# Laying out an attention kernel's instructions with measured durations and a new table of limits

## The chip, the cores and the metric

The kernel runs on one core of one Trainium2 chip. The metric is the time of one execution on the device in microseconds (us). The 48 executions of the kernel before that were taken beside the experiments lie between 832.57 and 835.77 us, all within 0.3% of their median (833.86), and all times compared here are of undisturbed ("fast") runs. One first execution of the kernel before, beside the result, took 1873.47 us and is left out of every comparison.

Short names in what follows: PE is the engine that runs the matmuls (PEld its weight loads, which overlap them: busy for 35% beside PE's 95%), ACT the one that runs most of the exponentials here, DVE and POOL the two that run the elementwise operations, SP the one that starts most transfers. "Line" numbers such as L1563 are those of the kernel's source.

## The reference

Two attention branches over the same input, mixed by a gate. Branch A is dense softmax attention with 2048 positions and 32 heads of width 20. Branch B looks at 8 positions, its own and 7 earlier ones, with a step of 2.

```python
def reference(A_x, A_wqkv, A_wo, B_x, B_wqkv, B_wo, gate_w):
    # _A_ref: q, k, v from x @ wqkv, 32 heads of 20
    #     p = softmax(q k^T * 20 ** -0.5);  (p v) @ wo
    # _B_ref: the same, but each position attends to idx = pos - 2 * (0..7)
    x = A_x                                   # [1, 2048, 640] bf16
    g = _sigmoid((x * gate_w).sum(-1, keepdims=True))
    a = _A_ref(x, A_wqkv, A_wo)
    b = _B_ref(x, B_wqkv, B_wo)
    return g * a + (1 - g) * b
```

Branch A sets the time (its visits, defined below, hold ACT for 790.7 of 831.5 us): 32 heads of 2048 x 2048 exponentials, cut into 2048 "tiles" of 128 x 512.

## The kernel before

Three notions carry everything below.

- A **visit** is one ACT instruction that exponentiates two or three score tiles from a score bank into `ebuf`.
- A **ride** is a tile that rides along in a visit's bank (or in a side bank), but is exponentiated by DVE: one operation makes `uD`, and for each group of up to four rides three shifted copies `eD` follow. PE then multiplies `uD` and the three copies with scaled values.
- A **filler** is a group of four matmuls that adds zeros or writes to a bank nobody reads. It is there to keep PE busy where PE has nothing to do; the granted clock with more and with fewer of them is measured in e4_hold_all (0.999 to 1.000) and e11_fewer_fillers (0.997 in two of four runs).

All instructions are put in order when the kernel is built, by an arithmetic that carries a clock for each engine. It decides at each step what comes next from where these clocks stand. It saves no instruction by itself: it only decides which tile becomes a ride, how many tiles a visit has and what stands between two visits. The durations and delays in the listing are what the layout assumes, not measurements.

```python
LAT = {"pe": 0.22, "act": 0.18, "dve": 0.13, "pool": 0.15, "sp": 0.1}   # assumed: end of a producer to start of a consumer, us
SWITCH = 0.11                                                         # assumed: PE changes its tiling

# in _Sched.task: the modelled start and end of an instruction
start = self.avail[stream]
for d in t.deps:
    start = max(start, d.end + LAT[d.stream])
# [cut: a rule for DVE beside POOL, PE's switch, transfers]
t.end = start + dur
self.avail[stream] = t.end

dvc = lambda n, mode=1: 0.10 + n * 1.0417e-3 / mode      # a generic DVE operation
actc = lambda n: 0.08 + n * 0.8334e-3                    # an ACT operation

# a visit
exps[s] = T("act", actc(512 * n), lambda e: e.activation(
    ebuf[s % NE][:, 0:512 * n], score[s % 2][:, 0:512 * n], ACTF.Exp, scale=LN2 / STEP), ...)

# a ride
t = T("dve", 0.69, lambda e: e.tensor_scalar(
    uD[d % 2][:, 512 * i:512 * (i + 1)].bitcast(I16), side[rb], UOFF, 0.0, op0=ALU.add, op1=ALU.max), ...)

# the shifted copies of a group of n rides, k = 1, 2, 3
T("dve", 0.11 + 0.1334 * n, lambda e, k=k, sl=sl: e.tensor_scalar(
    eD[:, sl % NS, 0:512 * n].bitcast(I16), uD[d % 2][:, 0:512 * n].bitcast(I16), SHIFTS[k], None, op0=ALU.add), ...)

# may the next tile ride?
idle = max(now, exps[s - 2].end + LAT["act"] if s > 1 else 0.0) + 0.4 - sch.avail["dve"]
if idle < -DWAIT:
    return None
# [cut: further conditions]

# side work and fillers of PE until the visit before has ended, plus a slack
lim = (exps[s - 1].end if s >= 1 else sch.avail["act"]) + SLACK[max(0, len(us) - 2)]
spend(lim)
```

The names `SLACK`, `DWAIT` and 17 more come from a table `PLAN`. A row takes effect at the visit whose number is its key and holds until the next row. The table before has 54 rows:

```python
PLAN = {
    0: ((0.32, 0.63), 0.32, 2.5, 2.5, 0.49, -1.0, -0.1, 11.8, 7.0, 7.2, 0.52, 0.47, 4.4, 4.0, 0.0, 0.85, 2, 5.5, 0.0),
    # [cut: 52 rows]
    720: ((0.37, 0.6), 0.13, 2.5, 1.0, 1.23, -1.03, -0.57, 12.37, 5.5, 8.26, 0.66, 0.46, 4.28, 4.75, 0.05, 0.72, 1, 0.0, 0),
}
```

Of the kernel before, what the change touches and what calls it, by code (L numbers as in the profile page):

```python
# [50 lines left out]
    0: ((0.32, 0.63), 0.32, 2.5, 2.5, 0.49, -1.0, -0.1, 11.8, 7.0, 7.2, 0.52, 0.47, 4.4, 4.0, 0.0, 0.85, 2, 5.5, 0.0),  # L51
    10: ((0.3, 0.64), 0.31, 2.5, 2.5, 0.49, -1.0, -0.1, 11.8, 7.0, 7.2, 0.52, 0.47, 4.4, 4.0, -0.32, 0.85, 2, 5.5, 0.0),
    20: ((0.3, 0.64), 0.27, 2.5, 1.0, 0.49, -1.0, -0.1, 11.8, 7.0, 9.93, 0.66, 0.47, 4.4, 4.0, -0.32, 0.85, 2, 5.5, 0.0),
    40: ((0.3, 0.61), 0.27, 2.5, 2.5, 1.15, -0.61, -0.1, 9.38, 7.0, 6.43, 0.52, 0.26, 4.34, 4.91, 0.0, 0.85, 3, 5.5, 0.0),
    60: ((0.27, 0.64), 0.29, 6.6, 6.3, 0.54, -1.02, -0.42, 9.46, 6.2, 6.34, 0.52, 0.47, 4.34, 2.59, 0.0, 0.85, 2, 2.5, 0.0),
    70: ((0.27, 0.64), 0.29, 6.6, 6.3, 0.54, -1.02, -0.42, 9.46, 4.5, 6.34, 0.52, 0.47, 4.34, 5.79, 0.0, 0.69, 2, 2.5, 1),
    80: ((0.27, 0.64), 0.29, 2.5, 6.3, 0.54, -0.4, -0.42, 9.38, 5.5, 6.34, 0.52, 0.47, 4.34, 2.59, 0.0, 0.85, 2, 2.5, -1.5),
    100: ((0.31, 0.7), 0.38, 2.5, 6.3, 0.54, -1.26, -0.42, 9.38, 5.5, 6.34, 0.52, 0.35, 4.34, 2.59, 0.0, 0.85, 2, 2.5, -1.5),
    120: ((0.27, 0.64), 0.33, 6.6, 6.3, 0.54, -1.02, -0.42, 9.46, 4.5, 8.77, 0.52, 0.46, 4.66, 5.79, 0.0, 0.65, 2, 2.5, -3),
    140: ((0.27, 0.64), 0.31, 6.3, 1.0, 0.54, -1.02, -0.42, 9.46, 4.5, 6.56, 0.52, 0.46, 3.47, 5.79, 0.0, 0.65, 1, 9.0, 0),  # L60
    150: ((0.25, 0.55), 0.31, 6.6, 1.0, 0.54, -1.02, -0.42, 9.65, 6.7, 6.56, 0.52, 0.46, 4.34, 5.79, 0.0, 0.65, 2, 9.0, 0),
    160: ((0.33, 0.47), 0.31, 6.6, 1.0, 0.54, -1.02, -0.42, 9.65, 5.5, 6.56, 0.52, 0.46, 4.34, 5.79, 0.0, 0.65, 1, 9.0, -3),
    170: ((0.33, 0.47), 0.31, 6.6, 1.0, 0.88, -1.02, -0.42, 9.65, 5.5, 6.56, 0.52, 0.46, 4.34, 2.17, 0.0, 0.65, 1, 0.0, -3),
    180: ((0.33, 0.47), 0.31, 6.6, 1.0, 0.88, -1.02, -0.42, 9.65, 5.5, 6.72, 0.52, 0.46, 4.34, 2.17, 0.0, 0.65, 1, 0.0, -1.5),
    200: ((0.33, 0.47), 0.31, 6.6, 1.0, 0.88, -1.02, -0.42, 9.65, 5.5, 9.72, 0.52, 0.46, 4.34, 2.17, 0.0, 0.65, 1, 0.0, -1.5),
    210: ((0.34, 0.46), 0.33, 2.5, 1.0, 0.63, -1.02, -0.42, 9.52, 7.0, 8.49, 0.68, 0.46, 5.15, 5.79, 0.0, 0.71, 2, 0.0, -3),
    240: ((0.34, 0.46), 0.35, 2.5, 1.0, 0.63, -1.02, -0.42, 9.74, 6.2, 6.12, 0.68, 0.46, 4.48, 5.79, 0.0, 0.77, 2, 6.6, -3),
    250: ((0.34, 0.46), 0.35, 2.5, 1.0, 0.63, -1.02, -0.42, 9.74, 6.2, 6.12, 0.68, 0.52, 4.48, 5.79, 0.0, 0.77, 2, 6.6, -3),
    260: ((0.34, 0.46), 0.33, 2.5, 1.0, 0.63, -1.02, -0.42, 9.52, 4.5, 8.49, 0.62, 0.46, 4.86, 5.79, 0.0, 0.61, 1, 6.6, -3),
    270: ((0.34, 0.46), 0.39, 1.0, 1.0, 0.63, -1.19, -0.42, 9.92, 6.2, 6.12, 0.68, 0.46, 4.48, 5.79, 0.0, 0.77, 2, 6.6, -3),  # L70
    290: ((0.34, 0.46), 0.39, 1.0, 1.0, 0.63, -1.19, -0.42, 12.33, 6.2, 6.12, 0.68, 0.37, 4.56, 5.88, 0.0, 0.77, 2, 6.6, -3),
    310: ((0.36, 0.5), 0.39, 1.0, 1.0, 0.65, -1.19, -0.42, 12.82, 6.2, 6.12, 0.68, 0.46, 4.48, 5.79, 0.0, 0.77, 2, 6.6, -3),
    320: ((0.36, 0.5), 0.39, 1.0, 6.6, 0.65, -1.19, -0.42, 9.92, 6.2, 7.5, 0.64, 0.46, 4.48, 5.79, 0.0, 0.77, 2, 6.6, -3),
    340: ((0.36, 0.5), 0.39, 1.0, 6.6, 0.61, -1.19, -0.42, 9.92, 6.2, 7.5, 0.68, 0.46, 4.48, 5.79, 0.0, 0.77, 2, 6.6, -3),
    350: ((0.36, 0.5), 0.05, 1.0, 6.6, 0.65, -1.19, -0.42, 10.62, 6.2, 7.5, 0.68, 0.46, 4.48, 5.79, 0.0, 0.77, 2, 6.6, -3),
    360: ((0.36, 0.5), 0.05, 1.0, 6.6, 0.65, -1.19, -0.04, 10.62, 4.5, 7.5, 0.68, 0.46, 4.48, 5.79, 0.0, 0.77, 1, 6.6, -3),
    380: ((0.34, 0.53), 0.05, 1.0, 6.6, 0.65, -1.19, -0.04, 10.62, 4.5, 7.5, 0.68, 0.46, 4.44, 5.79, 0.1, 0.77, 1, 6.6, -3),
    390: ((0.37, 0.49), 0.39, 1.0, 6.6, 0.65, -1.19, -0.42, 9.92, 6.2, 10.01, 0.68, 0.46, 4.48, 5.79, 0.0, 0.76, 2, 6.6, -3),
    400: ((0.42, 0.45), 0.39, 1.0, 2.5, 0.65, -1.19, -0.42, 9.92, 6.2, 10.01, 0.68, 0.46, 4.48, 5.79, 0.0, 0.76, 2, 6.6, -3),
    410: ((0.34, 0.53), 0.05, 1.0, 6.6, 0.65, -1.37, 0.11, 9.38, 4.5, 7.5, 0.68, 0.46, 4.44, 5.79, 0.1, 0.77, 2, 6.6, -3),  # L80
    420: ((0.3, 0.63), 0.07, 1.0, 6.6, 0.65, -1.19, -0.04, 10.62, 4.5, 7.5, 0.68, 0.46, 4.44, 2.04, 0.1, 0.77, 1, 9.0, -3),
    430: ((0.3, 0.63), 0.16, 1.0, 6.6, 0.65, -1.19, -0.95, 11.07, 7.0, 7.5, 0.68, 0.46, 4.44, 2.44, 0.1, 0.77, 1, 9.0, -3),
    460: ((0.3, 0.63), 0.16, 1.0, 1.0, 0.65, -1.51, -0.95, 11.07, 7.0, 9.31, 0.68, 0.46, 4.44, 2.44, 0.2, 0.77, 1, 2.5, 0),
    480: ((0.3, 0.63), 0.16, 1.0, 1.0, 0.65, -1.51, -0.95, 11.07, 7.0, 9.31, 0.68, 0.46, 4.44, 2.44, 0.2, 0.77, 1, 9.0, 0),
    490: ((0.35, 0.6), 0.07, 2.5, 6.6, 1.12, -0.96, -0.04, 12.37, 6.2, 7.85, 0.63, 0.46, 3.76, 5.79, 0.04, 0.67, 1, 5.5, 0),
    500: ((0.35, 0.6), 0.07, 2.5, 6.6, 1.12, -0.96, -0.57, 12.37, 6.2, 7.85, 0.63, 0.46, 4.28, 5.79, -0.03, 0.67, 1, 5.5, 0),
    510: ((0.35, 0.6), 0.07, 2.5, 6.6, 1.12, -0.96, -0.57, 12.37, 6.2, 7.85, 0.63, 0.46, 4.28, 5.79, -0.03, 0.67, 1, 0.0, -3),
    530: ((0.35, 0.6), 0.07, 2.5, 6.6, 1.12, -0.96, -0.57, 15.73, 6.2, 7.85, 0.63, 0.46, 4.28, 5.79, -0.03, 0.67, 1, 0.0, -3),
    540: ((0.35, 0.6), 0.07, 2.5, 6.6, 1.12, 0.16, -0.57, 15.73, 6.2, 7.85, 0.63, 0.46, 3.25, 5.79, -0.03, 0.67, 1, 0.0, -3),
    550: ((0.35, 0.6), 0.07, 2.5, 6.6, 1.12, -0.8, -0.57, 12.37, 6.2, 7.85, 0.6, 0.46, 4.28, 4.89, 0.05, 0.67, 1, 0.0, -3),  # L90
    560: ((0.34, 0.61), 0.07, 6.6, 6.6, 1.12, 0.16, -0.57, 15.73, 6.2, 7.26, 0.63, 0.44, 3.25, 3.16, -0.03, 0.67, 1, 2.5, -3),
    570: ((0.35, 0.62), 0.07, 6.6, 6.6, 1.12, 0.07, -0.57, 15.73, 6.2, 7.26, 0.36, 0.44, 3.25, 3.16, -0.03, 0.67, 1, 2.5, -3),
    580: ((0.35, 0.6), 0.07, 6.6, 6.6, 1.12, -0.96, -0.57, 12.37, 6.2, 7.85, 0.63, 0.46, 4.28, 5.79, -0.47, 0.76, 2, 0.0, -3),
    600: ((0.35, 0.6), 0.07, 2.5, 6.3, 1.12, -0.96, -0.57, 12.37, 6.2, 7.85, 0.63, 0.54, 4.28, 5.79, -0.47, 0.76, 2, 0.0, -3),
    610: ((0.3, 0.64), 0.32, 2.5, 2.5, 0.49, -1.0, -0.1, 11.17, 7.0, 7.2, 0.56, 0.47, 4.4, 3.16, 0.0, 0.85, 2, 5.5, 0.0),
    630: ((0.34, 0.56), 0.07, 2.5, 5.5, 1.12, -0.8, -0.57, 12.37, 6.2, 9.39, 0.69, 0.7, 4.28, 4.89, 0.05, 0.72, 1, 0.0, -3),
    640: ((0.37, 0.58), 0.07, 2.5, 5.5, 1.23, -0.95, -0.57, 12.37, 5.5, 10.86, 0.6, 0.46, 4.28, 4.89, 0.05, 0.72, 1, 0.0, -3),
    650: ((0.36, 0.58), 0.07, 2.5, 5.5, 1.12, -0.8, -0.57, 12.37, 6.2, 9.39, 0.6, 0.55, 4.28, 3.81, 0.09, 0.72, 1, 0.0, 0),
    670: ((0.35, 0.55), 0.07, 2.5, 5.5, 1.12, -0.8, -0.57, 8.92, 6.2, 9.39, 0.6, 0.55, 4.28, 3.81, 0.09, 0.72, 1, 0.0, 0),
    680: ((0.37, 0.6), 0.13, 2.5, 1.0, 1.6, -0.95, -0.57, 12.37, 4.5, 8.26, 0.44, 0.52, 4.29, 4.47, 0.05, 0.72, 1, 0.0, -3),  # L100
    690: ((0.37, 0.6), 0.13, 6.6, 1.0, 1.23, -0.95, -0.38, 12.37, 5.5, 8.26, 0.4, 0.43, 4.28, 4.47, 0.05, 0.76, 1, 0.0, 0),
    700: ((0.37, 0.6), 0.13, 6.3, 1.0, 1.6, -0.95, -0.57, 12.37, 5.5, 8.26, 0.54, 0.52, 6.07, 4.47, 0.05, 0.72, 2, 0.0, -3),
    710: ((0.26, 0.61), 0.13, 2.5, 1.0, 1.23, -0.95, -0.39, 12.37, 5.5, 8.26, 0.66, 0.59, 4.28, 4.47, 0.05, 0.72, 1, 0.0, 0),
    720: ((0.37, 0.6), 0.13, 2.5, 1.0, 1.23, -1.03, -0.57, 12.37, 5.5, 8.26, 0.66, 0.46, 4.28, 4.75, 0.05, 0.72, 1, 0.0, 0),
}
WEIGHTS = (1.0, 0.83984375, 0.70703125, 0.59375)
UOFF = 15992.765
K = len(SHIFTS)



LAT = {"pe": 0.22, "act": 0.18, "dve": 0.13, "pool": 0.15, "sp": 0.1}
SWITCH = 0.11
# [211 lines left out]
def _build(ctx, nc, A_x, A_wqkv, A_wo, B_wqkv, B_wo, gate_w, out):  # L325
# [1060 lines left out]

    BT0 = 230.0
    BT1 = 860.0
    BALL = 170.0
    DIDLE2 = -0.1  # L1390

    DWAIT = 0.49
# [410 lines left out]
```

## Time and profile before

| the kernel before | value |
|---|---|
| time, median of undisturbed runs | 833.5 us |
| span of the profiled run | 831.5 us |
| ACT busy, PE busy, DVE busy | 96%, 95%, 82% |
| visits (of three, two, one tile) | 726 (270, 455, 1) |
| tiles on ACT + rides | 1721 + 327 = 2048 |
| filler groups | 197 |

The prediction below shows the engine shares, the groups and the account of ACT. Two further views matter. The first is the chain of work that ended last, by line. Each share is the part of the span that the chain, followed back from the last instruction, spent in that line:

```profile
ACT ebuf L1563 44%; PE score L1540 12%; PE obank L1608 10%; PE side L562 9%; PE score L562 4%; PE obank L1629 1%; DVE eD L802 1%; PE score L1236 1%; PE obank L464 1%; ACT eB L919 1%; PE score L1629 0%; PE side L1629 0%; PE side L1259 0%; DVE uD L1553 0%; ACT tB L953 0%
```

The second is the list of waits: who waited, at which line, for whom, the sum in us, how often, and the longest.

```profile
PEld score L1540 <- ACT ebuf L1563: 142.8, 346, 1.2
...
PEld score L1540 <- DVE uD L1553: 20.5, 43, 0.9
...
PEld score L1540 <- DVE eD L802: 13.6, 34, 0.5
...
ACT ebuf L1563 <- PE score L1540: 7.9, 20, 2.1
```

### The profile page before, as it was taken

The numbers are of one execution on the slowest core, as the hardware profiler recorded it, in microseconds if no ns is written. First come the engines' busy times: TensorE is split into PE (matmuls) and PEld (weight loads), VectorE is DVE, ScalarE is ACT, GpSimd is POOL, SyncE is SP. The second block draws the span as 40 slices with busy tenths as digits, with TensorE's granted clock in tenths as the row PEclk, the third lists the DMA queues.
The fourth block names the chain that finished last, engine by engine and source line by source line (L and its number), as shares of the span: only waits on it lengthen the run. The fifth ranks groups of instructions, "written<-read, shape, count | busy, mean of one in ns | idle before, by whom it ended". The sixth has DMA issues, their size and how long they took to land.

```text
span 831.5 us, 29660 instructions
## 1 busy us (share of the span) xinstructions
PE 786.0 (95%) x12650; PEld 288.5 (35%) x12650; DVE 681.9 (82%) x1197; ACT 802.2 (96%) x758; POOL 133.6 (16%) x195
## 2 busy tenths in 40 slices
PE   8999999899899899999999999999989999998998
PEld 5332233333333342343234333333333333343233
DVE  7658887689788888978897898788988878988983
ACT  4999999999999999999999999999999999999995
POOL 5031014410111111011111012111101111011110
PEclk9999999999999999999999999999999999999999
DMA  9112111201111010011001011010011011000000
GB/s 311 34 30 51 40 36 34 66 5 28 30 38 33 12 42 20 13 35 34 19 21 44 14 21 35 13 42 28 11 31 29 11 31 29 24 28 18 24 6 35
DMA packets 45016, 29.15 MB, mean 35 GB/s; under 512 B 27204, under 2 KB 43684, under 8 KB 44884
## 3 DMA queue, kind: packets, MB, share of 16 engines
q1 hardware_dynamic: 44596, 26.92, 12.5%
q8 instruction: 100, 1.64, 0.8%
q10 hardware_dynamic: 288, 0.33, 0.1%
q14 instruction: 32, 0.26, 0.1%
HBM read 11.94 MB, written 2.62 MB: 18 GB/s over the span
## 4 chain that ended last, share of the span: by engine, by line
ACT 44%; PE 40%; issue 13%; DVE 3%; DVEq 0%; ACTq 0%
ACT ebuf L1563 44%; PE score L1540 12%; PE obank L1608 10%; PE side L562 9%; PE score L562 4%; PE obank L1629 1%; DVE eD L802 1%; PE score L1236 1%; PE obank L464 1%; ACT eB L919 1%; PE score L1629 0%; PE side L1629 0%; PE side L1259 0%; DVE uD L1553 0%; ACT tB L953 0%
## 5 line engine op out<-in xcount | busy, mean ns | idle before, releaser
L1563 ACT ACTIVATE ebuf<-score 128x1024 bf16<-128x1024 f32 (+1 forms) x726 | 790.7, 1232 | 9.8 <-PE score L1540 7.9
L1540 PE MATMUL score<-qT,kT 32*128 32x512 bf16 x2032 | 289.3, 384 | 33.1 <-ACT ebuf L1563 27.2
L1553 DVE TENSOR_SCALAR uD<-score 128x512 int16<-128x512 f32 x311 | 210.2, 685 | 53.7 <-PE score L1540 51.0
L802 DVE TENSOR_SCALAR eD<-uD 128x2048 int16<-128x2048 int16 (+1 forms) x246 | 170.9, 721 | 2.6 <-PE obank L1608 1.8
L1540 PEld LDWEIGHTS score<-qT,kT 32*128 32x128 bf16 x2032 | 73.0, 91 | 277.4 <-ACT ebuf L1563 142.8
L1608 PE MATMUL obank<-ebuf,vA 128*21 128x512 bf16 x1721 | 159.4, 385 | 2.1 <-ACT ebuf L1563 0.7
L562 PE MATMUL side<-xT,kvw 128*32 128x256 bf16 (+1 forms) x2440 | 100.4, 280 | 1.7 <-DVE rQ L956 0.7
L794 POOL TENSOR_TENSOR vS<-vA,vw 128x252 bf16<-128x252 bf16 x82 | 56.5, 692 | 270.3 <-PE obank L1608 229.6
L1608 PE MATMUL obank<-eD,vS 128*21 128x512 bf16 x981 | 86.6, 379 | 0.0
L562 PEld LDWEIGHTS side<-xT,kvw 128*32 128x32 bf16 x2440 | 57.4, 96 | 36.8 <-issue 20.4
L1608 PEld LDWEIGHTS obank<-ebuf,vA 128*21 128x21 bf16 x1721 | 37.8, 89 | 83.9 <-issue 72.2
L769 POOL TENSOR_TENSOR rcp<-rcp,gA 128x16 f32<-128x16 f32 x31 | 9.2, 298 | 325.9 <-DVE rcp L767 325.9
L975 DVE TENSOR_TENSOR stage<-qkvB,repB 128x1280 bf16<-128x1280 bf16 x64 | 50.7, 829 | 0.2 <-DMA repB<-eB 0.2
L874 DVE TENSOR_TENSOR stage<-qkvB 128x1280 bf16<-128x1280 bf16 x64 | 50.2, 818 | 0.2
L858 DVE CAST qkvB<-side 128x512 bf16<-128x512 f32 (+1 forms) x69 | 40.4, 594 | 9.9 <-PE side L562 9.4
L562 PE MATMUL side<-stage,ident 128*32 128x512 bf16 (+1 forms) x608 | 38.8, 348 | 0.1
L1629 PE MATMUL obank<-xT,zero 128*32 128x512 bf16 x424 | 34.8, 382 | 0.0
L775 POOL TENSOR_TENSOR oN<-oTt,rcp 128x512 bf16<-128x512 f32 x31 | 32.6, 1052 | 2.4
L1608 PE MATMUL obank<-uD,vA 128*21 128x512 bf16 x327 | 32.2, 379 | 0.0
L1608 PEld LDWEIGHTS obank<-eD,vS 128*21 128x21 bf16 x981 | 23.9, 91 | 16.0 <-issue 3.2
L562 PE MATMUL side<-woBp,oB 128*32 128x128 bf16 (+1 forms) x580 | 28.7, 293 | 0.7 <-DVE outsb L1113 0.5
L562 PE MATMUL side<-woA_d,oTd 128*32 128x128 bf16 (+1 forms) x580 | 28.8, 292 | 0.0
(178 smaller groups left out, 585.9 us busy)
## 6 DMA issues: line engine op xcount, KB each, us to landing
repB<-eB SPq DMA_DIRECT2D x128, 32.0 KB
WqP<-in_A_wqkv_dram SPq DMA_DIRECT2D x16, 160.0 KB
stage<-in_B_wqkv_dram SPq DMA_DIRECT2D x1, 2400.0 KB
oTd<-oN SPq DMA_DIRECT2D x108, 20.0 KB
qT<-dst SPq DMA_DIRECT2D x104, 20.0 KB
out_dram<-outsb SPq DMA_DIRECT2D x12, 160.0 KB
kvw<-in_A_wqkv_dram SPq DMA_DIRECT2D x2, 800.0 KB
oTd<-in_A_x_dram SPq DMA_DIRECT2D x2, 640.0 KB
```

The lines of the kernel that those rows point to most:

```text
L562: ins = e.matmul(o[j:k, :], l(j) if callable(l) else l[:, j:k], r, start=(first and i == 0), stop=(last and i == n - 1), skip_group_check= ...
L775: T(en, c2, lambda e: e.tensor_tensor(oo, ii, ib, ALU.mult), reads=["rcp", "oTt"], writes=["oN0"])
L794: T("pool", 0.7, lambda e: e.tensor_tensor(vS[:, d % 2, :, :], _ap(vA, (kb * NQ + q) * 4 * DV, [[0, K - 1], [1, 4 * DV]]), _ap(vw, 0, [[1, ...
L802: T("dve", 0.11 + 0.1334 * n, lambda e, k=k, sl=sl: e.tensor_scalar(eD[:, sl % NS, 0:512 * n].bitcast(I16), uD[d % 2][:, 0:512 * n].bitcas ...
L858: t = TB(dvc(n * TOK), lambda e, o=o, i=i: e.tensor_copy(o, i), reads=[("side", b)], writes=[key])
L874: TB(dvc(CN * TOK, 2), lambda e, w=w, ks=ks: e.tensor_tensor(prodB(w), qB[:, :, :], ks, ALU.mult), reads=["qB", "kB"], writes=[("prod", w) ...
L975: TB(dvc(CN * TOK, 2), lambda e, w=w, vs=vs, rr=rr: e.tensor_tensor(prodB(w), vs, rr, ALU.mult), reads=["vB", ("repB", w4 % NR)], writes=[ ...
L1540: ins = e.matmul(o, kT[32 * j:32 * j + 32, q, kb * P:(kb + 1) * P], qT[g % NQT][32 * j:32 * j + 32, :], start=True, stop=True)
L1553: t = T("dve", 0.69, lambda e: e.tensor_scalar(uD[d % 2][:, 512 * i:512 * (i + 1)].bitcast(I16), side[rb], UOFF, 0.0, op0=ALU.add, op1=ALU ...
L1563: exps[s] = T("act", actc(512 * n), lambda e: e.activation(ebuf[s % NE][:, 0:512 * n], score[s % 2][:, 0:512 * n], ACTF.Exp, scale=LN2 / S ...
L1608: ins = e.matmul(obank[32 * j:32 * j + DV, :], v, src, start=(kb == 0), stop=(last and k >= len(lst) - 4), skip_group_check=True)
L1629: ins = e.matmul(o[32 * j:32 * j + 32, :], w[:, 32 * j:32 * j + 32] if best else w[:, :], xT[:, 0, 0:512], start=bool(best), stop=bool(bes ...
```

## The change

The change alters numbers only. Its intent is that the layout knows the durations as the chip shows them, and that a search over the table's rows, looking ahead in the layout's arithmetic, then finds an order that ends sooner. The table has 55 rows after. The sum of a visit's fixed part and its delay to a reader stays 0.26, and the sum for a generic DVE operation stays 0.23: each gives to the delay what it takes from the duration.

```diff
 PLAN = {
-    0: ((0.32, 0.63), 0.32, 2.5, 2.5, 0.49, -1.0, -0.1, 11.8, 7.0, 7.2, 0.52, 0.47, 4.4, 4.0, 0.0, 0.85, 2, 5.5, 0.0),
+    0: ((0.41, 0.62), 0.32, 2.5, 2.5, 0.01, -1.0, -0.11, 11.8, 7.0, 7.2, 0.39, 0.47, 4.4, 2.32, 0.0, 0.85, 2, 5.5, 0.0),
 [cut: the other 53 rows before, 53 of the other 54 after]
+    710: ((0.43, 0.65), 0.13, 2.5, 1.0, 0.8, -0.6, -0.4, 13.8, 6.7, 7.01, 0.69, 0.57, 4.28, 5.98, 0.03, 0.69, 2, 6.6, 1),
 }
-LAT = {"pe": 0.22, "act": 0.18, "dve": 0.13, "pool": 0.15, "sp": 0.1}
+LAT = {"pe": 0.22, "act": 0.208, "dve": 0.163, "pool": 0.15, "sp": 0.1}
-    dvc = lambda n, mode=1: 0.10 + n * 1.0417e-3 / mode
-    actc = lambda n: 0.08 + n * 0.8334e-3
+    dvc = lambda n, mode=1: 0.067 + n * 1.0417e-3 / mode
+    actc = lambda n: 0.052 + n * 0.8334e-3
-            T("dve", 0.11 + 0.1334 * n, lambda e, k=k, sl=sl: e.tensor_scalar(
+            T("dve", 0.067 + 0.1334 * n, lambda e, k=k, sl=sl: e.tensor_scalar(
-    BALL = 170.0
+    BALL = 160.0
-            t = T("dve", 0.69, lambda e: e.tensor_scalar(
+            t = T("dve", 0.61, lambda e: e.tensor_scalar(
```

## The prediction

> **What bounds the kernel now.** I read the page's engine shares first, then its slices, its costliest groups, the windows by stage, the chain of waits, and last single instructions in the timeline.
>
> ```profile
> PE 786.0 (95%) x12650; PEld 288.5 (35%) x12650; DVE 681.9 (82%) x1197; ACT 802.2 (96%) x758; POOL 133.6 (16%) x195
> ACT  4999999999999999999999999999999999999995
> PEclk9999999999999999999999999999999999999999
> ACT 44%; PE 40%; issue 13%; DVE 3%; DVEq 0%; ACTq 0%
> L1563 ACT ACTIVATE ebuf<-score 128x1024 bf16<-128x1024 f32 (+1 forms) x726 | 790.7, 1232 | 9.8 <-PE score L1540 7.9
> L1553 DVE TENSOR_SCALAR uD<-score 128x512 int16<-128x512 f32 x311 | 210.2, 685 | 53.7 <-PE score L1540 51.0
> L802 DVE TENSOR_SCALAR eD<-uD 128x2048 int16<-128x2048 int16 (+1 forms) x246 | 170.9, 721 | 2.6 <-PE obank L1608 1.8
> ```
>
> ACT is busy in every slice but the first and last; almost all of it is one line, the exponentials of the scores, 726 "visits" of two or three score tiles of 512 columns. The clock is full throughout. The chain alternates between ACT and PE because a visit needs scores from PE, and PE needs the bank that the visit before last has read. A "ride" is a tile whose exponential DVE makes instead (L1553, then three shifted copies for a group of up to four rides, L802). There are 327 rides (311 here, 16 in a group with the other bank), so ACT has 2048 - 327 = 1721 tiles. That matches the count of matmuls that use ACT's results:
>
> ```profile
> L1563 ACT ACTIVATE ebuf<-score 128x1024 bf16<-128x1024 f32 x455 | 442.7, 1071 | 5.8 <-PE score L1540 4.0 <-ACT ebuf L1563 0.6
> L1563 ACT ACTIVATE ebuf<-score 128x1536 bf16<-128x1536 f32 x270 | 380.7, 1507 | 4.1 <-PE score L1540 3.8
> L1608 PE MATMUL obank<-ebuf,vA 128*21 128x512 bf16 x1721 | 159.4, 385 | 2.1 <-ACT ebuf L1563 0.7 <-DVE oTt L763 0.5 <-DVE eD L802 0.4
> L1553 DVE TENSOR_SCALAR uD<-side 128x512 int16<-128x512 f32 x16 | 11.0, 686 | 4.8 <-PE side L1540 4.6
> 19.70:820.40 800.70, 761.92 (x12375) 275.72 (x12371) 662.82 (x1154) 792.97 (x746) 121.36 (x174) 1.00 0.12 28
> ```
>
> Grouped by form: 455 visits of two tiles, 270 of three (one has one tile). The last line is the window from the first visit to the end of the last: 800.70 us, in which the columns are PE, weight loads, DVE, ACT and POOL busy. DVE has 138 us without work there.
>
> Durations overlap, so the real price of an instruction is the distance from its start to the next start. Single visits and single DVE instructions in the timeline:
>
> ```profile
> 689.24 1.05 ACT L1563 ACTIVATE ebuf<-score 128x1024 bf16<-128x1024 f32 x1
> 690.15 1.06 ACT L1563 ACTIVATE ebuf<-score 128x1024 bf16<-128x1024 f32 x1
> ```
>
> ```profile
> 440.01 0.69 DVE L1553 TENSOR_SCALAR uD<-score 128x512 int16<-128x512 f32 x1
> 440.62 0.68 DVE L802 TENSOR_SCALAR eD<-uD 128x2048 int16<-128x2048 int16 x1
> 441.21 0.69 DVE L1553 TENSOR_SCALAR uD<-score 128x512 int16<-128x512 f32 x1
> ```
>
> A visit of 1024 columns holds ACT for 0.91 us though it is recorded as 1.05; a ride holds DVE for 0.61 though recorded as 0.69; a shifted copy holds it for 0.59.
>
> [...]
>
> **An account of ACT.** Start until the first visit 19.7 us. [...] Fixed part: 726 x 0.051 = 37.0. Other small ACT work in the window, an estimate from their starts: 5. After the last visit: 831.5 - 820.4 = 11.1. The rest of the 800.7 window is waiting: 800.7 - 734.3 - 37.0 - 5 = 24.4 us. Only 9.8 of it appears as idle time, because the tail of the record before covers a short wait. So a better layout can gain in three places only: fewer tiles on ACT (0.427 us each), fewer visits (0.051 each), less of the 24.4.
>
> **The change part by part.** No operation is added or altered; the diff changes numbers by which the instruction order is laid out when the kernel is built.
>
> First, the layout's idea of durations. A visit's fixed part goes from 0.08 to 0.052 (measured about 0.051), its visibility delay from 0.18 to 0.208, so that the sum stays 0.26. A generic DVE operation goes from 0.10 to 0.067 fixed, a ride from 0.69 to 0.61 (measured 0.61), a shifted copy of four from 0.644 to 0.601 (measured 0.59). On the chip this saves nothing by itself. But the layout now sees DVE free earlier: 327 x 0.08 = 26.2, plus 246 x 0.043 = 10.6, plus some 450 other operations that use the generic formula (counted over their rows) x 0.033 = 14.9, together some 52 us. A further ride costs DVE 0.61 + 3/4 x 0.60 = 1.06 us, so 52 us would hold 49 more rides. The layout also sees ACT finish 726 x 0.028 = 20 us sooner, so it puts less side work of PE between two visits than it did.
>
> Second, the table per ten visits. It decides how far DVE may lag when a ride is opened (fifth number; 1.11 from visit 370 on, before only from 490), how far PE may overrun (first pair), and filler limits. I can't read a time out of 19 numbers by 56 rows. One bound I can read: its last row is at visit 710, and rows are only made for visits that exist, so there are at least 711 visits. With V visits, tiles = 2 V + (visits of three) + rides = 2048, so rides + visits of three are at most 2048 - 1422 = 626, against 327 + 270 = 597 now. If the visits of three stay, at most 29 rides come in; if these fall, as rides in a score bank push out the third tile, more can.
>
> Third, the pace of branch B's work (170 to 160) follows its shorter modelled durations and should move nothing.
>
> The sum, by my choice: 20 more rides, about two fifths of the 49 that the freed model time would hold, because a ride also needs a free bank and the old table already had a ride threshold to tune: -20 x 0.427 = -8.5 us; 10 visits fewer: -0.5; ACT's waits from 24.4 to some 21, since release times are now modelled as they are: -3. Together -12.0, so 833.5 - 12 = **821.5 us**. Start and tail (19.7 and 11.1) stay.
>
> **The rivals.** (1) PE becomes the bound. It is 95% busy, each extra ride gives it three further passes of a quarter group (a group of four takes about 0.215, an estimate from its recorded starts), 0.16 us, 20 rides 3.2 us; the late rows let PE overrun by up to 0.52 against 0.37 before. Against it: 788 matmuls of the filler line L1629 are 197 groups, some 42 us by that estimate, which are dispensable. If it holds, ACT's waits grow by what the rides save: 828 to 836. (2) DVE becomes the bound: rides are accepted while DVE lags by over 1 us, the score bank is then released late, and PE's next scores wait (PE's weight loads for scores already wait 20.5 us for rides in the list of waits). For it is the laxer middle; against it the 138 us of DVE without work. It would make 826 to 832. (3) The freed time is used in full: 49 rides, -20.9, visits -1.2, waits -3, giving some 808; with 29 rides -12.4 - 0.8 - 3, giving 817. DVE would rise by 31 to 52 us of its 138 idle, which is possible, but the old table was tuned to the same end. (4) The search fitted its own model and the chip scatters: no gain, 833.
>
> **Range and chances.** Most weight lies on 10 to 30 more rides, hence 817 to 828. Range 811 to 831. Faster by over 2% means below 816.8, which needs about 30 rides with the waits cut, or 40 without: 0.22. Slower by over 2% needs 850, against which the durations that now match the trace speak: 0.03. Same: 0.75.
>
> **What would show the steps right or wrong.** Rides: the count of L1553 should be some 347 and the matmuls from ACT's results some 1701. Visits: about 716. DVE busy should rise by some 20 us to about 703. Waits: the account above, redone on the new trace, should leave about 21 us. Fillers should fall. The fixed part of a visit and the distance of ride to next start must stay at 0.05 and 0.61. I am wrong if rides stay below 335 (the freed DVE time was not used), or if ACT's waits grow past 27 us (PE or DVE took over), or if rides pass 360.

The data term of the account of ACT, 734.3 us, which the account subtracts, the trace gives: at the closest the next visit starts 0.904 us after a visit of two and 1.331 us after a visit of three, so a tile is 0.427 us (0.4267 from the means), 1721 tiles are 734.3 us, and 0.051 us remain as a visit's fixed part. The forecast's sum: -8.5 - 0.5 - 3 = -12.0, and 833.5 - 12.0 = 821.5 us.

## More of the kernel before

PE waits mostly for ACT to free a score bank (142.8 us in 346 waits). It waits for a ride's DVE operation 43 times. DVE hardly appears in the chain at all.

## The result

The kernel after took 836.55 us (median of 835.67, 835.77, 837.32 and 838.28), the kernel before 833.55 us beside it. The ratio is 1.0041, with a 95% interval of 1.0017 to 1.0065. Here and below a ratio is the mean time of one kernel's fast runs over that of the other's of the same rounds, so it is not quite the ratio of the medians quoted. By the 2% rule the two are the same; the change did not gain, and it lost about 0.4%.

In the kernel after, the line L1563 is L1564, because the table grew by one row. The page of the kernel after, engine shares, ACT's slices, the chain by engine and by line, and the groups that answer to those shown of before:

```profile
PE 786.4 (94%) x12601; PEld 289.8 (35%) x12601; DVE 682.6 (82%) x1191; ACT 803.2 (96%) x755; POOL 138.0 (16%) x194
...
ACT  4999999999999999999999999999999999999995
...
ACT 42%; PE 34%; issue 13%; DVE 9%; SPq 1%; DMA 1%; DVEq 0%; ACTq 0%
ACT ebuf L1564 42%; PE score L1541 10%; PE obank L1609 9%; PE side L563 7%; PE score L563 3%; DVE uD L1554 2%; DVE eD L803 2%; PE obank L1630 2%; SPq L710 1%; DVE qkvB L859 1%; DVE stage L976 1%; DVE stage L875 1%; PE side L891 1%; PE score L1237 1%; DMA oTd<-in_A_x_dram 1%
...
L1564 ACT ACTIVATE ebuf<-score 128x1024 bf16<-128x1024 f32 (+1 forms) x723 | 791.4, 1250 | 15.7 <-PE score L1541 13.6
...
L1554 DVE TENSOR_SCALAR uD<-score 128x512 int16<-128x512 f32 x304 | 204.2, 682 | 51.0 <-PE score L1541 49.4
L803 DVE TENSOR_SCALAR eD<-uD 128x2048 int16<-128x2048 int16 x243 | 170.1, 725 | 3.5 <-PE obank L1609 2.3
...
L1609 PE MATMUL obank<-ebuf,vA 128*21 128x512 bf16 x1724 | 158.9, 386 | 3.8 <-ACT ebuf L1564 1.7
```

Three things stand here. The work is all but the same: 1724 tiles on ACT, so 324 rides (304 here and 20 in the side bank), 723 visits, DVE busy 682.6 us. ACT's idle time before its visits grew from 9.8 to 15.7 us. And in the chain PE fell from 40 to 34% while DVE rose from 3 to 9%: DVE has come into the path without having more work.

The groups of visits by form, the side-bank rides, and the window from the first visit to the last (columns: length, then PE, weight loads, DVE, ACT and POOL busy, granted clock, share of transfers, GB/s):

```profile
L1564 ACT ACTIVATE ebuf<-score 128x1024 bf16<-128x1024 f32 x443 | 429.4, 1082 | 11.9 <-PE score L1541 10.3 <-PE side L563 0.3
L1564 ACT ACTIVATE ebuf<-score 128x1536 bf16<-128x1536 f32 x279 | 390.8, 1518 | 3.6 <-PE score L1541 3.2
L1554 DVE TENSOR_SCALAR uD<-side 128x512 int16<-128x512 f32 x20 | 13.6, 681 | 3.7 <-PE side L1541 3.6
18.80:826.40 807.60, 764.31 (x12369) 278.42 (x12366) 664.41 (x1149) 794.00 (x743) 125.70 (x173) 1.00 0.12 28
```

With these the account of ACT can be redone. Data is tiles x 0.4267 us (to rounding; the smallest distance to the next start is 1.331 us after a visit of three and 0.904 us after one of two), the fixed part is visits x 0.0507 us (0.9041, the mean of the smallest distances after a visit of two, less two tiles), and the waits are what remains. The third column is a run described below (label e4_hold_all), in which the clock of the kernel after was held up.

| us | before | after | after, clock held |
|---|---|---|---|
| until the first visit | 19.7 | 18.8 | 19.8 |
| data | 734.3 | 735.6 | 735.6 |
| fixed part of visits | 36.8 | 36.7 | 36.7 |
| other small ACT work (an estimate) | 5.1 | 5.1 | 5.1 |
| waits | 24.4 | 30.1 | 27.3 |
| after the last visit | 11.1 | 9.9 | 9.9 |
| span (to rounding) | 831.5 | 836.3 | 834.5 |

The waits carry the difference. The list of waits of the kernel after shows part of it:

```profile
PEld score L1541 <- ACT ebuf L1564: 135.1, 323, 1.2
...
PEld score L1541 <- DVE uD L1554: 30.3, 66, 0.8
...
ACT ebuf L1564 <- PE score L1541: 13.6, 26, 2.2
...
PEld score L1541 <- DVE eD L803: 6.2, 19, 0.5
```

PE's score matmuls now wait 66 times for a ride to clear its bank, not 43, and ACT waits 26 times for scores, not 20. But their waits for shifted copies fell, from 34 to 19. Over all operations of DVE, the weight loads for scores waited about 52 us before and about 56 after (sums of the list's lines). So the list alone doesn't show that DVE holds PE much longer; that DVE costs more in the new order rests on the chain, and on e12_dve_load_new below.

There is one more thing, which the slices of the profile's page hide, since each is 20.9 us long. Two of the four runs of the kernel after had a mean granted clock of 0.998 (838.28 and 837.32 us), and two of 1.000 (835.77 and 835.67 us). In the profiled run, windows of 3.4 us (columns as above) show this:

```profile
769.00:772.40 3.40, 1.77 (x46) 0.72 (x46) 0.00 (x0) 3.40 (x5) 0.61 (x1) 1.00 0.06 14
772.40:775.80 3.40, 3.19 (x38) 1.28 (x38) 1.87 (x5) 2.53 (x4) 0.00 (x0) 0.50 0.19 51
```

From 769.0 to 772.4 PE was busy for about half of the time (1.77 of 3.40 us), and then it ran at a granted clock of 0.50 for 3.41 us. That the light stretch before it is the cause is a guess at this point, which e3_hold_clock and e4_hold_all put to the test.

### The profile page after: what moved, and what is told of

It reads as the page before. It is cut to its first block, busy times and chain, and to the rows that moved or that the text cites. A ratio compares the mean times of both kernels' runs of the same rounds, so it can differ in the third digit from the quotient of the medians.

```text
span 836.3 us, 29557 instructions
## 1 busy us (share of the span) xinstructions
PE 786.4 (94%) x12601; PEld 289.8 (35%) x12601; DVE 682.6 (82%) x1191; ACT 803.2 (96%) x755; POOL 138.0 (16%) x194
## 4 chain that ended last, share of the span: by engine, by line
ACT 42%; PE 34%; issue 13%; DVE 9%; SPq 1%; DMA 1%; DVEq 0%; ACTq 0%
ACT ebuf L1564 42%; PE score L1541 10%; PE obank L1609 9%; PE side L563 7%; PE score L563 3%; DVE uD L1554 2%; DVE eD L803 2%; PE obank L1630 2%; SPq L710 1%; DVE qkvB L859 1%; DVE stage L976 1%; DVE stage L875 1%; PE side L891 1%; PE score L1237 1%; DMA oTd<-in_A_x_dram 1%
## 5 line engine op out<-in xcount | busy, mean ns | idle before, releaser
L1564 ACT ACTIVATE ebuf<-score 128x1024 bf16<-128x1024 f32 (+1 forms) x723 | 791.4, 1250 | 15.7 <-PE score L1541 13.6
L1554 DVE TENSOR_SCALAR uD<-score 128x512 int16<-128x512 f32 x304 | 204.2, 682 | 51.0 <-PE score L1541 49.4
L803 DVE TENSOR_SCALAR eD<-uD 128x2048 int16<-128x2048 int16 x243 | 170.1, 725 | 3.5 <-PE obank L1609 2.3
L795 POOL TENSOR_TENSOR vS<-vA,vw 128x252 bf16<-128x252 bf16 x81 | 59.4, 735 | 271.5 <-PE obank L1609 235.8
L563 PE MATMUL side<-xT,kvw 128*32 128x256 bf16 (+1 forms) x2500 | 102.6, 281 | 1.6 <-DVE qkvB L859 1.2
L1609 PE MATMUL obank<-eD,vS 128*21 128x512 bf16 x972 | 83.9, 379 | 0.0
L875 DVE TENSOR_TENSOR stage<-qkvB 128x1280 bf16<-128x1280 bf16 x64 | 53.5, 869 | 0.1
L563 PE MATMUL side<-stage,ident 128*32 128x512 bf16 (+1 forms) x736 | 45.2, 345 | 0.3
L1630 PE MATMUL obank<-xT,zero 128*32 128x512 bf16 x444 | 36.5, 385 | 0.0
L764 DVE STREAM_TRANSPOSE oTt<-obank 128x512 f32<-128x512 f32 x32 | 22.7, 708 | 5.8 <-PE obank L1609 5.5
L563 PE MATMUL side<-woA_d,oTd 128*32 128x512 bf16 (+1 forms) x440 | 24.1, 308 | 0.0
```

The costliest lines, as they stand in the source:

```text
L563: ins = e.matmul(o[j:k, :], l(j) if callable(l) else l[:, j:k], r, start=(first and i == 0), stop=(last and i == n - 1), skip_group_check= ...
L795: T("pool", 0.7, lambda e: e.tensor_tensor(vS[:, d % 2, :, :], _ap(vA, (kb * NQ + q) * 4 * DV, [[0, K - 1], [1, 4 * DV]]), _ap(vw, 0, [[1, ...
L803: T("dve", 0.067 + 0.1334 * n, lambda e, k=k, sl=sl: e.tensor_scalar(eD[:, sl % NS, 0:512 * n].bitcast(I16), uD[d % 2][:, 0:512 * n].bitca ...
L875: TB(dvc(CN * TOK, 2), lambda e, w=w, ks=ks: e.tensor_tensor(prodB(w), qB[:, :, :], ks, ALU.mult), reads=["qB", "kB"], writes=[("prod", w) ...
L1554: t = T("dve", 0.61, lambda e: e.tensor_scalar(uD[d % 2][:, 512 * i:512 * (i + 1)].bitcast(I16), side[rb], UOFF, 0.0, op0=ALU.add, op1=ALU ...
L1564: exps[s] = T("act", actc(512 * n), lambda e: e.activation(ebuf[s % NE][:, 0:512 * n], score[s % 2][:, 0:512 * n], ACTF.Exp, scale=LN2 / S ...
```

## The experiments

Twelve kernels were run on the chip, each beside the kernel before. The names in the expectations are theirs; where an expectation speaks of the layout's "arithmetic", that is the end which the kernel's own layout code works out for itself. It is no time of the chip, and is used here only to say what the layout believes.

What the layout believes is worth stating first. By its own arithmetic the last visit of the kernel before ends so that the whole is 834.5, and of the kernel after 820.6, a gain of 13.9. But if the instruction order of the kernel before is priced again with the new durations, it ends at 821.6. So 12.9 of the 13.9 are a different price of the same order, and 1.0 is a better order. What each part is worth on the chip is what the runs below ask.

### The table and the durations apart

e1_old_table: the kernel after with the old table.

```diff
 PLAN = {
-    [cut: the 55 new rows]
+    [cut: the 54 old rows]
 }
```

> The changed kernel with the old table of layout numbers put back, so the new durations alone. Theory A (table and durations are fitted to each other, neither holds a gain by itself): the layout falls apart, by 2% or more slower than before, 850 to 875 us, with fewer rides than 327 (some 311) and more waits of ACT. Rival B (the exact durations are the gain, and the new table spoils it): 820 to 832 us, with rides above 327. Rival C (the durations hardly matter, the layout is robust): 831 to 838 us.

Measured: 874.17 us (872.21 to 874.87) beside 833.83, ratio 1.0477 (1.0463 to 1.0491). The row of ACT's slices and the chain:

```profile
ACT  4996999799999999999998999999999999989991
...
PE 40%; ACT 37%; issue 12%; DVE 9%; DMA 1%; SPq 1%; POOL 0%; DVEq 0%; ACTq 0%; POOLq 0%
```

ACT has holes (sixes to eights among the nines), and the account gives 311 rides and 50.7 us of waits. The clock was down too, to 0.989 to 0.992: the profiled run spent 17.1 us at half clock before its last 3 us, some 8.5 us of PE's work, where 40 us were lost.

e2_new_table: the kernel before with the new table.

```diff
 PLAN = {
-    [cut: the 54 old rows]
+    [cut: the 55 new rows]
 }
```

> The kernel before with the new table alone; durations and pace of branch B as before. Theory A: slower than before by 2% or more, 850 to 870 us, some 315 rides. Rival B' (the new table is the gain, the exact durations take it back): 820 to 832 us. Rival C: 831 to 838 us.

Measured: 864.77 us (864.24 to 865.65), ratio 1.0372 (1.0357 to 1.0387), with 316 rides and 50.2 us of waits. The clock was 0.993 to 0.996, with 6.8 us at half clock in the profiled run before its last 4 us, some 3.4 us of PE's work, where 31 us were lost.

What follows: the layout's arithmetic foresaw both losses, since it ends at 857.1 for e1_old_table and at 861.8 for e2_new_table. The likely reason is that a row of the table belongs to one visit of one particular order: with other durations the same visit number falls on another state of the engines, and the limits no longer fit. Neither part of the change can be had alone, and the 0.4% of the whole is not the sum of two independent effects.

### The half clock

e3_hold_clock: six extra filler groups around the light window, where PE was waiting anyway.

```diff
         def fn(e):
+            for j in list(range(4)) * (4 if s == 677 else 0):
+                e.matmul(obank[32 * j:32 * j + 32, :], zero[:, :], xT[:, 0, 0:512], start=False, stop=False, skip_group_check=True)
...
+        reps = 3 if s == 676 and not best else 1
-            for j in range(4):
+            for j in list(range(4)) * reps:
```

> The changed kernel with six more filler groups on PE (two beside the filler in front of visit 677, four after the scores of visit 677), where the profile shows PE busy for 1.77 of 3.40 us and then 3.41 us at half clock; order and everything else unchanged, 12625 matmuls for 12601. If the light stretch of PE causes the half clock, every run has clock 1.000 and the kernel takes 835.5 to 836, without the runs at 837 to 838. If the half clock comes from elsewhere, some runs stay at 0.998 and 837 to 838. In both cases it stays 2 us slower than before, since the clock explains only part of the difference.

Measured: 837.19 us (836.36 to 839.95), ratio 1.0043 (1.003 to 1.0056). The dip at 772 us was gone, but the profiled run had one at 627 us and a clock of 0.998. That all runs would be at 1.000 was a miss: the kernel has several light stretches, and half clock came at 772.4 us in the profiled run of the kernel after and at 627 us in this one. The time was a miss as well: even the one run at 1.000 took 837.96, not 835.5 to 836. Why is open; the added groups may cost time themselves.

e4_hold_all: the kernel after with 34 filler groups (the page counts 136 matmuls more; the expectation says 33) ahead of fourteen visits, at all of its light stretches. The layout counts no time for them, so the order of everything else is unchanged.

```diff
+    EXTRA = {125: 2, 374: 2, 412: 4, 440: 2, 550: 2, 555: 1, 618: 2, 668: 3, 674: 3, 676: 2, 677: 2, 678: 4, 688: 2, 694: 3}
+
+    def hold_clock(n):
+        [cut: n groups of four matmuls that add zeros]
+        T("pe", 0.0, fn, reads=["zero", ("xT", 0, 0)], accum=["obank"], mode=sch.mode)
...
+            if EXTRA.get(s) and obank_free <= sch.avail["pe"]:
+                hold_clock(EXTRA[s])
```

> The changed kernel with filler groups in front of the scores of fourteen visits (33 groups in all), wherever its trace has PE idle for 0.3 us or more inside a stretch of 3.4 us in which less than 0.43 of the array was used; order of everything else unchanged. [...] Theory D (light stretches of PE cause the half clock, which costs about 2 us each time): every run at clock 1.000 and at 835 to 836 us, no run over 836.5, ratio to before 1.002 to 1.003. Rival (the half clock has another cause): runs at 0.998 remain and the median stays at 837. If fillers delay the scores that follow them, the time rises by up to 1 us though the clock is 1.000.

Measured: 836.38 us (835.57 to 836.68) beside 833.84, ratio 1.0027 (1.0014 to 1.0041). The profiled run has no half clock before the very end. The expectation was met nearly: three of the five runs read 0.999, not 1.000, and one took 836.68, not 836.5 or less.

```profile
ACT 42%; PE 35%; issue 12%; DVE 11%; DVEq 0%; ACTq 0%
...
L1564 ACT ACTIVATE ebuf<-score 128x1024 bf16<-128x1024 f32 (+1 forms) x723 | 791.4, 1255 | 13.0 <-PE score L1541 10.8
```

What follows: with the clock held, the kernel is still slower, its waits are still 27.3 us, and DVE still stands in the chain. The half clock is worth about 1.2 us of the mean (1.0041 - 1.0027, times 834). The two intervals overlap, so this run alone doesn't prove it, and the two states of the clock have to be compared within one kernel. The runs of the kernel after average 837.8 us where the clock was 0.998 and 835.7 where it was 1.000, half of them each. The kernel before gives a larger sample: of its 48 executions beside these experiments, five had a clock of 0.998 and took 835.1 to 835.8 us, and the other 43 took 832.6 to 835.0, on average 1.8 us less. So the kernel before isn't free of the half clock; it falls into it less often. The rest of the difference, 2.2 to 2.5 us, belongs to the order: the two runs of the kernel after at 1.000, which have no added fillers, lie 2.2 us above the kernel before.

### Is it the arithmetic that is still too crude?

e5_cal_table: the layout got a delay for each pair of engines, landing times for transfers and a few durations as the traces of before and after show them, and a table that was searched anew on these.

```diff
-SWITCH = 0.11
+SWITCH = 0.120
+EDGE = {("pe", "act"): 0.275, ("pe", "dve"): 0.215, ("pe", "pool"): 0.26, ("act", "pe"): 0.230, [cut: eight more]}
+LAND = {("qTd", 3): 4.6, ("qTd", 7): 6.7, ("qTd", 8): 7.3, [cut: fifteen more]}
...
-            start = max(start, d.end + LAT[d.stream])
+            start = max(start, d.end + (0.05 if d.dom == "dma" else EDGE.get((d.stream, stream), 0.15)))
[cut: a few durations, and 62 table lines in place of 55]
```

> A third layout: the changed kernel with the layout arithmetic corrected further (delay from PE to ACT 0.275 for 0.22, a switch of PE hidden behind a wait, 0.012 us more for each group of scores and of outputs, landing times of the transfers as in the traces, the two tiny groups on PE at 0.03 and 0.12), and a table found for that arithmetic by trying 150 rows at every tenth visit and keeping what ends first. Its arithmetic ends at 832.2 us, with 317 rides and 720 visits; the changed kernel's arithmetic ended at 820.6 and the chip took 833.7 to 836.3. Theory E (what the changed kernel's arithmetic lacked are delays outside the ACT and DVE durations): the measured span lies within 4 us of 832.2. Theory F (a layout drifts by 10 us or more whatever the arithmetic, since the waits that add up are chance): span of 840 us or more. Neither expects it to beat 833.5 by over 1%.

Measured: 841.97 us (841.39 to 843.11), ratio 1.0094 (1.0077 to 1.0111); spans 839.2 to 841.3 where the arithmetic said 832.2. The one expectation, within 4 us of the arithmetic, was missed; the other, 840 or more, was met by three of the four spans, and only by a little. Better single delays did not make this searched order keep its promise: the chip took 7 to 9 us back. A likely reason, argued and not shown, is that the search finds an order that uses up whatever the arithmetic gives away. My search was short, so this is a case against "the arithmetic was only off by a few constants", not a proof that no search can win.

### What a microsecond on each engine is worth

The prediction's main step priced a tile off ACT at its full 0.427 us, and DVE's and PE's extra work at nothing. These runs measure the three prices one by one, on the kernel before. A price here is the change of the kernel's time for each us of work that is added to an engine or taken off it.

e6_tiles_off: every twelfth visit of three exponentiates only two of its tiles, so ACT has 21 tiles fewer, 21 x 0.427 = 9.0 us, with no ride in their place. The result is wrong (those tiles use old data).

```diff
+    third = [0]
...
+        m = n
+        if n == 3 and s > 60:
+            third[0] += 1
+            m = 2 if third[0] % 12 == 0 else 3
-            ebuf[s % NE][:, 0:512 * n], score[s % 2][:, 0:512 * n], ACTF.Exp, scale=LN2 / STEP),
+            ebuf[s % NE][:, 0:512 * m], score[s % 2][:, 0:512 * m], ACTF.Exp, scale=LN2 / STEP),
```

> The kernel before, order unchanged, in which every twelfth visit of three tiles after visit 60 works on two tiles only, 20 or 21 tiles in all (result wrong on purpose). It prices a tile taken off ACT. If ACT is the bound, as the prediction counted, each tile gives 0.427 us back: 21 tiles, 9.0 us, 824 to 826 us. If PE paces the layout and ACT waits instead, less than half comes back: 829 to 833 us.

Measured: 829.84 us beside 833.53, ratio 0.9959 (0.9941 to 0.9978). That is 3.7 us for 9.0, a **price of 0.41**. The waits rose from 24.4 to 30.9 us: more than half of what ACT saved came back as waiting. In the list of waits, those of visits for scores rose from 7.9 to 12.0 us, and in the chain PE now leads:

```profile
PE 44%; ACT 40%; issue 10%; DVE 3%; DMA 1%; SPq 1%; DVEq 0%; ACTq 0%
```

e7_dve_load: 35 DVE operations of about 0.60 us each, 21 us, that nobody needs, and that the layout counts as no time, so the order stays.

```diff
+            if sl % 7 == 3:
+                T("dve", 0.0, lambda e: e.tensor_reduce(
+                    kmx4[:, 0:1], uD[d % 2][:, 0:512], AX.X, ALU.max, apply_absolute_value=True),
+                  reads=[("uD", d % 2, 0)], writes=[("kmx4", 0)])
```

> The kernel before, order unchanged, with 35 more DVE operations of 0.60 us each (a maximum over a ride's 512 columns, result unused) behind every seventh shifted copy: 21 us, the DVE load of 20 more rides. It prices that load. If DVE's 138 us without work can take it, as the prediction counted, the time rises by at most 2 us, 833.5 to 835.5. If DVE is close to the path (late rides hold score banks), by 4 to 10 us, 838 to 844.

Measured: 836.37 us beside 833.53, ratio 1.0035 (1.0019 to 1.0051). That is 2.8 us for 21, a **price of 0.13**, between the two expectations (at most 2, or 4 to 10).

e8_both: the edits of e6_tiles_off and e7_dve_load together, which is what 20 more rides would do to ACT and DVE, PE left out.

> Both at once: the ACT relief and the DVE load of 20 more rides, without PE's share (result wrong on purpose). The prediction's conversion says 825 to 828 us, 6 to 9 below before. If the conversion doesn't pay even at fixed order, 833 us or more.

Measured: 837.09 us (832.9 to 838.49), ratio 1.0034 (1.0005 to 1.0062). Three of the four runs had a clock of 0.996 to 0.998. The one nearest full clock (0.999) took 832.9, where the two single effects add to 833.5 - 3.7 + 2.8 = 832.6. As far as one run can tell, the effects add, and less ACT work for more DVE work in this ratio gained 0.6 us, before PE's share of a ride is counted. The gain of 6 to 9 us that the prediction's conversion gives came in none of the four.

e9_pe_load: 28 filler groups more, four matmuls each, 28 x 0.215 = 6.0 us of PE, one after every twelfth group of matmuls into the output bank, wherever that fell.

```diff
+        npvc[0] += 1
+        more = npvc[0] % 12 == 0 and not last and len(tiles) > 60
...
+            for j in range(4 if more else 0):
+                ins = e.matmul(obank[32 * j:32 * j + 32, :], zero[:, :], xT[:, 0, 0:512], start=False, stop=False, skip_group_check=True)
```

> The kernel before, order unchanged, with 28 more groups of filler on PE ([...]6.0 us in all, 12762 matmuls for 12650), one behind every twelfth output group. It completes the prices: e6 gave back 0.41 of the 9.0 us taken off ACT, e7 charged 0.13 of the 21 us put on DVE. Theory G (PE and ACT share the path, so PE's time costs about what ACT's relief lacked): 0.4 to 0.7 of 6.0 us, 836 to 838 us. Rival (PE has slack, the missing relief is lost in waiting for something else): under 0.15 of it, 833.5 to 834.5 us.

Measured: 835.71 us beside 833.86, ratio 1.0024 (1.0009 to 1.0039). That is 1.85 us for 6.0, a **price of 0.31**, again between the two expectations (0.4 to 0.7, or under 0.15).

What follows from the three: the prices of ACT, PE and DVE are 0.41, 0.31 and 0.13. With the intervals of the ratios they are 0.20 to 0.55, 0.12 to 0.54 and 0.08 to 0.20, so ACT and PE can't be told apart, and DVE is the cheapest, as its share in the chain of before suggests (44, 40 and 3%). A share is no price, though: DVE's is 0.13 where its share is 3%. And all three are far from the busy shares (96, 95 and 82%).

e10_fewer_fillers: can the fillers pay for rides? 88 of the 197 filler groups were cut to one small matmul, chosen so that every 3.4 us stays well filled. That is 88 x 0.215 = 19 us of PE.

```diff
+    CUT = {1, 4, 6, 8, 19, 26, 27, 35, 36, [cut: 79 more]}
...
+            if cut:
+                return e.matmul(o[0:32, 0:64], w[:, 0:32], xT[:, 0, 0:64], start=bool(best), stop=bool(best), skip_group_check=True)
```

> The kernel before, order unchanged, with 88 of its 197 filler groups cut to one tiny matmul, 18 us of PE, chosen where no idle time of PE follows before the next scores and where every stretch of 3.4 us keeps a use of the array over 0.40. Theory G: PE relieved by 18 us at 0.3 to 0.6 gives 5 to 10 us: 823 to 829 us, faster than both kernels. Rival: the scores wait for ACT anyway, 832 to 834 us. Where the cut makes a light stretch after all, runs with a clock of 0.996 to 0.998 appear and 2 us are lost each time.

Measured: 833.01 us (832.84 to 833.31) beside 833.86, ratio 0.9991 (0.9976 to 1.0006): inside the noise. At 0.31 the cut should have given 5.8 us. The layout puts a filler only where PE would wait, so removing one gives a wait in its place: matmuls and weight loads for scores waited 186.4 us for visits in this run's profile (150.9 + 35.5), and 170.0 in that of before (142.8 + 27.2). A price measured by adding work at arbitrary places does not hold for taking away work that sits in gaps.

e11_fewer_fillers: the same on e4_hold_all, 90 of 187 groups.

```diff
+    CUT = {1, 2, 4, 5, 7, 9, 10, 11, 12, 13, [cut: 80 more]}
```

> The same for the changed kernel with the fillers of e4 kept: 90 of 187 filler groups cut, 19 us of PE. Theory G: 826 to 831 us. Rival: 835 to 836.5 us, as e4.

Measured: 836.2 us (834.32 to 837.37), ratio 1.0033 (1.0017 to 1.005). Two runs had a clock of 0.999 and 1.000 (834.32 and 835.5), two of 0.997 (836.89 and 837.37). With fewer fillers the clock fell again, and the run decides nothing.

### Has DVE lost its slack?

e12_dve_load_new: the 35 useless DVE operations of e7_dve_load, put into e4_hold_all, that is, into the new order with its clock held. If the padded durations of the kernel before were a margin, the same 21 us must cost more here.

```diff
+            if sl % 7 == 3:
+                T("dve", 0.0, lambda e: e.tensor_reduce(
+                    kmx4[:, 0:1], uD[d % 2][:, 0:512], AX.X, ALU.max, apply_absolute_value=True),
+                  reads=[("uD", d % 2, 0)], writes=[("kmx4", 0)])
```

> The DVE load of e7 (35 operations, 21 us) put into the changed kernel, with the fillers of e4 so that the clock stays up. e4 stood at a ratio of 1.0027 to before. Theory H (with every DVE operation laid out 0.03 to 0.08 us shorter, the new order leaves DVE less room, as the chain's DVE share of 9% for 3% suggests): the load costs clearly more than the 2.8 us it cost before, 5 us or more, ratio 1.0085 or above. Rival (the order has as much room as before): 2 to 4 us, ratio 1.005 to 1.0075.

Measured: 844.65 us (843.72 to 844.92) beside 835.01, ratio 1.0112 (1.0095 to 1.0129). Against e4_hold_all, each taken over the kernel before of its own rounds, that is (1.0112 - 1.0027) x 834 = 7.1 us for 21, a **price of 0.34, where the order before had 0.13**. With the intervals it is 0.25 to 0.43 against 0.08 to 0.20. Three of the seven executions of the kernel before beside it had a clock of 0.998, so 0.34 is low if anything. The page:

```profile
PE 795.5 (94%) x12735; PEld 291.3 (35%) x12737; DVE 700.6 (83%) x1226; ACT 805.3 (96%) x755; POOL 137.1 (16%) x194
...
PE 37%; ACT 32%; DVE 20%; issue 10%; DMA 1%; POOL 0%; DVEq 0%; ACTq 0%
```

DVE is busy for 83%, which looks like room. It holds 20% of the chain; with the same addition in the old order (e7_dve_load) it held 9%. The profiled run had one window at half clock (at 478.7 us), which cannot explain it: the three runs at 1.000 took 843.72 to 844.91. So the new order, with its fillers, leaves DVE less room. That the lost padding is the reason, and not the table, isn't shown: the load was not put into e1_old_table or e2_new_table.

## Why the prediction was wrong

**The failed step** is "20 more rides, about two fifths of the 49 that the freed model time would hold: -20 x 0.427 = -8.5 us". It failed twice.

First, the rides did not come: 324, three fewer than before, against an expected 347, and DVE was busy for 682.6 us, not 703. The prediction named this itself as a sign of being wrong ("if rides stay below 335"). The 52 us that DVE seemed to gain in the arithmetic were the old durations' padding, and the new table turned none of it into rides.

Second, they would not have paid. At the measured prices 20 rides take 8.5 x 0.41 = 3.5 us off by ACT, and add 20 x 1.06 x 0.13 = 2.8 us by DVE and 3.2 x 0.31 = 1.0 us by PE: together +0.3 us. Within the intervals of the prices it is anything from a gain of about 2.6 to a loss of about 4.2 us, and far from -8.5. e8_both, the first two together on the chip, shows no gain either, though three of its four runs also lost clock. So the old kernel stood near a balance, where a tile costs about the same on ACT as on DVE and PE. That this balance is why the search added none is argued, not shown: the search worked on the arithmetic, not on the chip. A full search that is forced to more rides was not run, and that question stays open.

**The step on waits** ("release times are now modelled as they are: -3") had the wrong sign: they rose by 2.9 us with the clock held (24.4 to 27.3), 5.7 in the profiled run. e12_dve_load_new points to why: the price of a disturbance on DVE went from 0.13 to 0.34. The old numbers overcharged a visit by 0.028 us and a DVE operation by 0.03 to 0.08 us. That was wrong as a duration, and it seems to have been useful as a margin. The layouts of four kernels, all priced with the new durations, speak for it. Of the two orders that were laid out with the old durations, the kernel before should end at 821.6 and e2_new_table at 852.3; their profiled spans were 9.9 and 10.1 us longer. Of the two laid out with the new durations, the kernel after should end at 820.6 and e1_old_table at 857.1; they were 15.7 and 15.1 us longer. With either table, then, the order without padding lost 5 to 6 us more to what the arithmetic doesn't know. Half clock explains some 2 us of this for the kernel after, but for the pair e1 and e2 it could explain all of it (17.1 us at half clock against 6.8), so the margin is likely and not proved. One place where the chip leaves the layout is visible in both traces: shifted copies while POOL copies weights. The arithmetic has a rule for this (it starts one of the two after the other has ended), and in both layouts these copies don't meet; on the chip the times have slipped, and they do.

```profile
58.38 6.97 POOL L820 COPY kvw<-stage 128x640 bf16<-128x640 bf16 x5
...
64.11 1.79 DVE L802 TENSOR_SCALAR eD<-uD 128x2048 int16<-128x2048 int16 x1
```

```profile
61.03 7.76 POOL L821 COPY kvw<-stage 128x640 bf16<-128x640 bf16 x5
...
65.14 2.43 DVE L803 TENSOR_SCALAR eD<-uD 128x2048 int16<-128x2048 int16 x2
...
67.63 0.40 PE L1609 MATMUL obank<-ebuf,vA 128*21 128x512 bf16 x4 [1.13 <-DVE eD L803]
```

These are single instructions in the timeline (start, length, then the instruction and the idle time before it), before and after. The copy beside POOL took 1.79 us where the mean is 0.72. After, the two took 2.43 us together, one of them 1.83, so the meeting itself cost about the same; but PE waited 1.13 us for it, where before a weight load had waited 0.36. Why a copy takes longer beside POOL was not shown. Some operations of both engines became a little longer on average in the new order, and nothing shows the reason for that either:

```profile
L794 POOL TENSOR_TENSOR vS<-vA,vw 128x252 bf16<-128x252 bf16 x82 | 56.5, 692 | 270.3 <-PE obank L1608 229.6
...
L874 DVE TENSOR_TENSOR stage<-qkvB 128x1280 bf16<-128x1280 bf16 x64 | 50.2, 818 | 0.2
```

```profile
L795 POOL TENSOR_TENSOR vS<-vA,vw 128x252 bf16<-128x252 bf16 x81 | 59.4, 735 | 271.5 <-PE obank L1609 235.8
...
L875 DVE TENSOR_TENSOR stage<-qkvB 128x1280 bf16<-128x1280 bf16 x64 | 53.5, 869 | 0.1
```

The same POOL operation went from a mean of 692 to 735 ns, the same DVE operation from 818 to 869. Set against the layout's own clock, the last visit of the kernel before came 4.2 us earlier than laid out, and that of the kernel after 14.8 us later (some 2 of it from the half clock). Of the 19.0 us between these, 13.0 are only the new price of the same order (by the new durations, the last visit of the kernel before ends at 811.5 instead of 824.5). The other 6.0 us are new lag. Which of the unmodelled delays make up the lag is open; e5_cal_table, which put several of them into the arithmetic, did not bring the lag of its span below 7.

**What was not foreseen at all** is the half clock, about 1.2 us of the mean. The prediction read "the clock is full throughout" from the profile of before and carried it over. A measure that ranks the windows is array use, an estimate: each matmul's columns, at 2370 per us (in the trace of before, filler groups of four matmuls of 512 columns follow each other at 0.216 us), times the share it takes of 128 x 128, the largest form in these traces, over 3.413 us, the length of the recorded half clock. In windows that line up with that half clock, and with each matmul's work put at the start of its record, the kernel after has 0.30 at 769.0 (the dip followed) and 0.32 at 472.0 (none followed); the lightest of the profiled run of before has 0.37. With the work put at the end of the record the order turns: 0.36 at 769.0 against 0.35 at 472.0. A threshold doesn't come out of these traces.

**What was right.** The prices that it said must stay did: the start of a visit still follows that of a visit of two by 0.904 us at the closest, and a ride still holds DVE for 0.60 us. Fillers fell as it said, from 197 groups to 187. The tail moved by about 1 us; the start moved no more than chance moves it (18.8 to 19.8 us in runs of the new order). That "same" came true is partly luck: the gain of 12 us that was forecast also lies inside the 2%. Rival (1), PE as the bound, and rival (2), DVE, each named part of it: they gave 826 to 836, where the result lies just above. Neither engine became *the* bound, though: three engines share the chain. Rival (4), a search that fitted its own model, is the closest in mechanism: 12.9 of the modelled gain of 13.9 was a new price for the old order, and its time, 833, was within 0.4% of the result. It deserved more weight. e1_old_table and e2_new_table show how tightly table and arithmetic are fitted to each other.

**One version to take away?** No kernel with a right result beats the kernel before. e10_fewer_fillers is at 0.9991, inside the noise.

## What to carry to other kernels

Price a microsecond by the chain that ended last and by a run that adds or removes a known amount, not by an engine's busy share: here ACT was busy for 96% and worth 0.41, DVE was busy for 82% in both kernels and worth 0.13 in one and 0.34 in the other. When a static order is laid out on modelled durations, ask what the padding in them was covering before it is removed, and first price the old order with the new numbers: the gain that is left after that is all the search has really found. And look at granted clock in windows as short as the half clock recorded here, 3.41 us, since a page's slices (20.9 us here) can hide a dip.
